# A recurrent-convolution and gated-MLP kernel: loads spread over two queues, four roots on ScalarE, a dummy Silu, eight banks for products and a new written order

## The chip, the cores and the metric

The kernel runs on one core of a Trainium2 chip. Its engines work side by side and meet through semaphores: TensorE (PE in the profile; its weight loads are PEld), VectorE (DVE), ScalarE (ACT), GpSimd (POOL) and SyncE (SP), which here only issues DMAs. ScalarE issues some DMAs too (ACTq). The metric is the device time of one execution in microseconds (us). Times are compared by the median of the runs of one kernel. The profile is of one execution, and its times count from the first instruction of the span.

## The reference

The input x is 2048 rows of 512, in bf16. What is computed:

```python
xn = layernorm(x)                                   # over the 512 columns
k_shift = sum_t  k[row - t, :] * shift_k[:, t]      # four taps
kv  = k_shift * v
y   = irfft(rfft(kv, 4096) * rfft(ssm_k, 4096))[:2048] + kv * ssm_D     # per column
s   = xn * y
h   = gelu(xn @ w_gate) * (xn @ w_up)               # 512 -> 1792
g   = silu(h @ w_down)                              # 1792 -> 512
out = x + s * g
```

## The kernel before, in words

**The MLP.** The rows are in four quarters (q0 to q3) of 512 rows, four row tiles each. For every quarter and each of 14 chunks of 128 hidden columns, a *unit* makes two products of four matmuls (gate and up, line 649), a Gelu on ScalarE (line 1216) and a multiplication on VectorE, either from PSUM (line 1225) or, where ScalarE first copies up out of PSUM, from SBUF (line 1222). The *down* product of a row tile is 14 matmuls in three pieces (4, 5, 5). For q0 to q2 a Tanh (line 1257) and a multiplication (line 1259) follow, which make the Silu and write G; the last quarter is done with the Silu itself (line 1265). The order of the quarters is q0, q1, q3, q2 with parts of q3 mixed in.

**The norm.** For each row tile VectorE takes statistics (lines 872, 873). For tiles 0 and 1, ScalarE takes a root (line 885) and VectorE the reciprocal (886); for tiles 2 and 3, and for the later quarters, GpSimd takes a power of -0.5 (line 889). q0 is transposed by TensorE; q1 to q3 by a transposing DMA on SyncE's queue (line 911, `xnT<-XN`).

**The convolution** is a transform over 4096 points in two stages, as matrix products. The filter (Hn) is loaded in four pieces; VectorE transposes each (line 940). TensorE makes the first stage of the filter in eight *H* stages (line 980), each of which takes four PSUM banks; ScalarE copies out, VectorE adds (line 988), and ScalarE's queue stores to DRAM (ZH). For the input, VectorE makes the four taps per quarter with 2048-wide operations (lines 1028, 1032, 1034) and multiplies by v (line 1036, `V<-KAC,V`, the *V piece*); the taps' weights are copied by GpSimd (line 1009, SKB). Sixteen *K* products (line 969) follow, and their stores (ZK) on SyncE's queue. The second stages run on 32 x 32 tiles (line 1051): eight of the filter, eight of the input, eight *inverses*, each with two aligned pairs of banks. The inverses are stored (ZI) and read back (BI) once all are there, then eight last products (y, line 1300) and the tail on VectorE (lines 1309, 1317, 1329, 1267, 1268). The table of the second stage (TF) is made by GpSimd: two products (line 755), a sum (758), four turned copies (642, 643); it also does one small *fold* (947).

**The order.** All work is cut into 801 numbered tasks. The string SEQ gives the order in which they are written; a task goes to the list of its engine, or with the letter b to its second choice, and each engine works its list in order. Semaphore waits are derived from what a task reads and writes. Loads are tasks too, each in the queue that its line names. LAND holds assumed landing times; with them the builder works out which PSUM bank a task gets, and nothing else depends on them. PSUM has eight banks: products take single ones (pool `psF`, at most NF_BANKS at a time), the transforms aligned pairs.

Numbers of the tasks that the prediction names: 14, 15 the two table products; 16 their sum; 76 the turned copies; 127 to 130 the tap copies; 54 the fold; 454, 455, 456 variance, power and bias of q1; 138, 146, 154, 162 the V pieces; 206 to 208 and the like the K stages; 125, 90, 110 the additions and 126, 91, 111 the stores of H stages 7, 0, 4; 652 to 658 variance to normalised rows of q3, 659 its transposing DMA; 560 to 566 and 567 the same of q2; 732, 735, 741 three of the multiplications of line 1309; 345 the last inverse; 13 the row copies of FT; 75 the table of Gelu.

GpSimd's list before: 2 4 3 5 70 73 127 130 129 128 455 54 14 15 16 76 653 561.

Of the kernel before, what the change touches and what calls it, by code (L numbers as in the profile page):

```python
# [26 lines left out]
SEQ = (  # L27
# [23 lines left out]
)  # L51
NF_BANKS = 4
ISSUE = 470.0
LAND = {"x0_0": 3350, "x0_1": 3900, "wg0": 5000, "wu0": 5700, "x0_2": 6200, "wg1": 7900, "wu1": 9400, "h0": 10700, "h1": 12000, "wg2": 13500, "wu2": 15000, "h2": 16300, "h3": 17600, "D": 18000, "kz": 10800, "x1": 19500, "sk": 21500, "kh1": 23000, "kh113": 23200, "k0": 24600, "wg3": 26100, "wu3": 27600, "k1": 29000, "wd0": 31800, "k2": 33200, "wd1": 35700, "v0": 37200, "v1": 38600, "k3": 40000, "v2": 41400, "v3": 42700}
W_XT, W_SW, W_BK, W_BH, W_ZI, W_BI, W_ZK, W_MI, W_G1 = 850000, 690000, 685000, 688000, 310000, 575000, 600000, 329000, 150000
# [5 lines left out]
N_SPLIT = 2  # L61
N_ROOT = 2
UNITS = [(0, 6), (0, 8), (0, 10), (0, 12), (1, 0), (1, 2), (1, 4), (1, 6), (1, 8), (1, 10), (1, 12), (1, 1), (1, 3), (1, 5), (1, 7), (1, 9), (1, 11), (1, 13)]
# [357 lines left out]
def build_kernel(nc, A_q, A_k, A_v, A_shift_k, A_ssm_k, A_ssm_D, B_w_gate, B_w_up, B_w_down, out):  # L421
    with ExitStack() as es0:
# [100 lines left out]
        trk = Trk(nc, block)  # L523
# [21 lines left out]
        R_id = res("ident", ident[:])  # L545
        R_cols, R_col1, R_col2 = (res(f"COLS{i}", COLS[:, i:i + 1]) for i in range(3))
        R_st = [res(f"st{t}", stats[:, t, :]) for t in range(NT)]
# [78 lines left out]
        def load(name, out_ap, in_ap, w_res, w_buf, nbytes, ring="SP", r=(), rb=()):  # L626
            sem = dsem("d_" + name)
            last_load[0] = S.add([("loads", ISSUE)], lambda e: dma(ring, out_ap, in_ap, sem, r, w_res), r=rb, w=w_buf, nbytes=nbytes, land=float(LAND[name]))

# [133 lines left out]
        def gelu_table(e):  # L763
            trk.op("ACT", lambda h: h.activation(COLS[:, 1:2], COLS[:, 0:1], ACTF.Gelu_apprx_tanh), r=[R_cols], w=[R_col1])

        def sines(e):
            sin(F1, C32[:].rearrange("p a c -> p (a c)"), [R_C32], R_F1)
            sin(TAB[:], PH[:], [R_PH], R_TAB)
            gelu_table(e)
# [51 lines left out]
        def load_x0(t):  # L821
            ts = slice(*((0, 1), (1, 2), (2, 4))[t])
            load(f"x0_{t}", X[:, ts, :], x_dr[:, ts, :], R_X[ts], bX[0][ts], 131072 * (ts.stop - ts.start))

# [5 lines left out]
        def load_h(k, ring):  # L830
            load(f"h{k}", Hn[:, k, :], h_dr[:, k, :], [R_Hn[k]], [bHn[k]], 524288, ring)
# [28 lines left out]
        for what in ORDER.split():  # L860
            if what[0] == "x" and len(what) == 3:
                load_x0(int(what[2]))
                continue
            {"k": load_k, "v": load_v, "w": lambda i: load_w(i, ("ACT", "ACT") if i == 0 else ("SP", "SP")), "x": load_x, "d": load_wd, "h": lambda i: load_h(i, "SP"), "s": load_taps, "D": load_d}[what[0]](int(what[1:]))

# [65 lines left out]
        d_out = []  # L931
        gu_tasks = [[] for _ in range(NQ)]
        down_tasks = [[] for _ in range(NQ)]

# [253 lines left out]
        def unit(q, m):  # L1188
# [10 lines left out]
            if q == 0 and m < N_HALF:  # L1199
# [15 lines left out]
            gu_tasks[q] += [tg, tu]  # L1215
            op([("ACT", act(512))], lambda e, h: h.activation(GE[:, g.slot, :], bank(pg), ACTF.Gelu_apprx_tanh), r=[pg], w=[g],  # L1216
               rr=lambda: R_bank(pg), ww=lambda: [R_GE[g.slot]], after=[t_gelu] if q == 0 else [])
            af = (down_tasks[q - 2] if q >= 2 else []) + (s1_tasks["H"] if q == 1 else [])
# [9 lines left out]
        def down(q):  # L1228
            for jt in range(4):
                t = 4 * q + jt  # L1230
                cols = [(0, DM)] if t < NT - 1 else [(0, 384), (384, DM)]
                for c0, c1 in cols:
# [23 lines left out]
                    if q < NQ - 1:  # L1256
                        op([("ACT", act(n))], lambda e, h, g=g, pc=pc: h.activation(g, pc(), ACTF.Tanh, scale=0.5), r=[p], w=[bt],  # L1257
                           rr=lambda p=p: R_bank(p), ww=rg, after=h_tr_tasks + (h2_tasks if q >= 2 else []))
                        op([("DVE", dve(512, 1))], lambda e, h, g=g, pc=pc: h.scalar_tensor_tensor(out=g, in0=g, scalar=1.0, in1=pc(), op0=ALU.add, op1=ALU.mult),
                           r=[p, bt], w=[bG[t // 2]], rr=lambda p=p, rg=rg: R_bank(p) + rg, ww=rg)  # L1260
                        continue
# [3 lines left out]
                    op([("ACT", act(n))], lambda e, h, g=g, pc=pc: h.activation(g, pc(), ACTF.Silu), r=[p], w=[bt],  # L1265
                       rr=lambda p=p: R_bank(p), ww=rg, after=zh_tasks + h2_tasks)
                    op([("DVE", dve(n, 2))], lambda e, h, g=g, u=u: h.tensor_tensor(g, g, u, ALU.mult), r=[bt, bS[t // 2]], w=[b2], rr=rg + [R_XN[t]], ww=rg)
# [36 lines left out]
        for j in range(8):  # L1304
# [6 lines left out]
            else:  # L1311
# [6 lines left out]
               rr=lambda by=by, R_g=R_g: [R_BO[by.slot], *R_g], ww=R_g)  # L1318

        down(NQ - 1)  # L1320


# [64 lines left out]
```

## Time and profile before

| | |
|---|---|
| median of 3 runs | 189.59 us (189.29 to 191.28) |
| profiled execution | 189.26 us, span 187.4 us |
| TensorE busy | 178.4 us (95%) |
| VectorE busy | 172.5 us (92%) |
| ScalarE busy | 138.4 us (74%) |
| GpSimd busy | 19.6 us (10%) |
| granted TensorE clock | 1.0 in every slice |

A row of a timeline reads: start in us, busy us, engine, line, operation, what is written `<-` what is read, partitions x elements and type, count, and in brackets the idle time just before it and what ended that. A row of waits reads: engine, line `<-` what it waited for: us in all, times, longest. A row of windows reads: the window, its length, the busy time of the engine with its count, the granted clock, the DMA share and GB/s. Operations of one engine overlap a little at their ends, so that the step from one start to the next is about 0.1 us shorter than the busy time.

### The profile page before, as it was taken

How to read it: one execution, taken by the hardware profiler on the slowest of the kernel's cores; microseconds unless marked ns; L12 is line 12 of the kernel's file. 1: busy time of each engine (PE TensorE's matmuls, PEld its weight loads, DVE VectorE, ACT ScalarE, POOL GpSimd, SP SyncE). 2: the span in 40 equal slices, each digit the busy share in tenths (PEclk: the TensorE clock that was granted, in tenths of full speed). 3: DMA queues.
4: the chain of work that ended last, by engine and by line, in shares of the span. 5: the costliest groups of instructions: out<-in, count | busy, mean ns of one | idle time of the engine just before them, and what ended most of it. 6: DMA issues, size and time to landing. Idle time of an engine off the chain costs nothing.

```text
span 187.4 us, 3808 instructions
## 1 busy us (share of the span) xinstructions
PE 178.4 (95%) x1522; PEld 77.8 (42%) x1522; DVE 172.5 (92%) x251; ACT 138.4 (74%) x200; POOL 19.6 (10%) x31
## 2 busy tenths in 40 slices
PE   8699999989499999999999999999999999999993
PEld 3464444344244433343443443343333434445552
DVE  5898999999999999999778999999999998769995
ACT  3697797985387999987847479798887977451771
POOL 4200135991000000002200000000000000000000
PEclk9999999999999999999999999999999999999999
DMA  5999999999756689357979959689942416599248
GB/s 164 337 373 403 317 364 366 405 352 223 237 205 243 229 286 287 132 191 259 292 220 283 320 205 327 220 263 286 351 159 115 168 59 224 162 371 394 98 153 284
DMA packets 38684, 48.38 MB, mean 258 GB/s; under 512 B 9484, under 2 KB 28428, under 8 KB 38667
## 3 DMA queue, kind: packets, MB, share of 16 engines
q1 hardware_dynamic: 31082, 39.23, 65.3%
q10 hardware_dynamic: 7584, 8.91, 13.5%
q8 instruction: 12, 0.20, 0.4%
q14 instruction: 6, 0.04, 0.1%
HBM read 27.39 MB, written 14.68 MB: 225 GB/s over the span
## 4 chain that ended last, share of the span: by engine, by line
PE 66%; DVE 21%; DMA 6%; SPq 3%; POOL 2%; issue 1%; DVEq 0%
PE psall L649 55%; DMA Hn<-in_A_ssm_k_dram 6%; PE psall L1051 6%; DVE KTM L1032 3%; SPq L622 3%; DVE KAC L1034 3%; PE psall L969 2%; DVE G L1329 2%; DVE G L1317 2%; DVE HTr L940 2%; PE psall L1246 2%; POOL mv L889 2%; DVE HT L1225 1%; DVE HT L1222 1%; DVE X L988 1%
## 5 line engine op out<-in xcount | busy, mean ns | idle before, releaser
L649 PE MATMUL psall<-xnT,Wg 128*128 128x512 bf16 (+1 forms) x248 | 56.6, 359 | 0.0
L649 PE MATMUL psall<-xnT,Wu 128*128 128x512 bf16 (+1 forms) x248 | 56.3, 359 | 0.2 <-ACT xnT L640 0.2
L649 PE MATMUL psall<-Wd,HT 128*128 128x512 bf16 (+1 forms) x182 | 40.3, 368 | 0.9 <-DVE HT L1225 0.9
L1216 ACT ACTIVATE GE<-psall 128x512 bf16<-128x512 f32 x54 | 31.6, 608 | 11.7 <-PE psall L649 10.0
L649 PEld LDWEIGHTS psall<-xnT,Wu 128*128 128x128 bf16 x248 | 22.5, 98 | 26.4 <-issue 1.3
L649 PEld LDWEIGHTS psall<-xnT,Wg 128*128 128x128 bf16 x248 | 21.6, 98 | 26.5 <-issue 3.8
L1225 DVE TENSOR_TENSOR HT<-psall,GE 128x512 bf16<-128x512 f32 x36 | 24.2, 682 | 5.5 <-PE psall L649 5.1
L649 PEld LDWEIGHTS psall<-Wd,HT 128*128 128x128 bf16 x182 | 16.2, 98 | 21.5 <-issue 2.5
L640 ACT ACTIVATE BO<-psall 128x1024 bf16<-128x1024 f32 x19 | 19.0, 1028 | 6.0 <-PE psall L1051 3.2
L1154 DVE TENSOR_TENSOR HSW<-KB,HSW 128x2048 bf16<-128x2048 bf16 x16 | 19.5, 1218 | 0.4 <-ACT KB L640 0.3
L640 ACT ACTIVATE HSW<-psall 128x1024 bf16<-128x1024 f32 x15 | 14.6, 1030 | 3.0 <-PE psall L1051 1.8
L640 ACT ACTIVATE KB<-psall 128x1024 bf16<-128x1024 f32 x14 | 14.0, 1035 | 3.7 <-PE psall L1051 3.7
L1032 DVE TENSOR_TENSOR KTM<-KK,SKB 128x2048 bf16<-128x2048 bf16 x12 | 15.3, 1272 | 0.0
L1034 DVE TENSOR_TENSOR KAC<-KAC,KTM 128x2048 bf16<-128x2048 bf16 x12 | 14.8, 1237 | 0.1
L1246 PE MATMUL psall<-Wd,HT 128*64 128x512 bf16 (+1 forms) x112 | 12.5, 366 | 0.0
L889 POOL TENSOR_TENSOR mv<-mv,NHALF 128x4 f32<-128x4 f32 (+1 forms) x5 | 6.1, 1212 | 58.8 <-DVE mv L883 53.4
L872 DVE BATCH_NORM_STATS2 stats<-X 128x6 f32<-128x512 bf16 x16 | 10.6, 677 | 1.1 <-DMA X<-in_A_q_dram 1.0
L1257 ACT ACTIVATE G<-psall 128x512 bf16<-128x512 f32 x12 | 7.1, 599 | 6.0 <-PE psall L649 5.5
L640 ACT ACTIVATE X<-psall 128x1024 bf16<-128x1024 f32 x8 | 8.2, 1028 | 4.0 <-PE psall L980 3.9
L640 ACT ACTIVATE U__73<-psall 128x512 bf16<-128x512 f32 x18 | 10.9, 617 | 0.3 <-PE psall L649 0.3
L640 ACT ACTIVATE AST<-psall 128x1024 bf16<-128x1024 f32 x10 | 10.1, 1029 | 1.1 <-PE psall L969 0.9
L1154 DVE TENSOR_TENSOR KB<-KB,HSW 128x2048 bf16<-128x2048 bf16 x8 | 9.6, 1219 | 0.1
(95 smaller groups left out, 189.7 us busy)
## 6 DMA issues: line engine op xcount, KB each, us to landing
BH<-ZH SPq DMA_DIRECT2D x8, 512.0 KB, 4.4
HSW<-HSW SPq DMA_DIRECT2D x16, 256.0 KB, 2.7
BK<-ZK SPq DMA_DIRECT2D x8, 512.0 KB, 6.0
ZI<-BO ACTq DMA_DIRECT2D x16, 256.0 KB, 2.5
BI<-ZI SPq DMA_DIRECT2D x8, 512.0 KB, 8.1
ZK<-AST SPq DMA_DIRECT2D x6, 512.0 KB, 3.0
Hn<-in_A_ssm_k_dram SPq DMA_DIRECT2D x4, 512.0 KB, 9.1
KK<-in_A_k_dram SPq DMA_DIRECT2D x4, 512.0 KB, 11.9
```

The lines of the kernel that those rows point to most:

```text
L640: return h.activation(o, i, ACTF.Copy, scale=scale)
L649: return h.matmul(o, lhsT=l, rhs=r, start=st, stop=sp)
L872: t_stats[t] = op([("DVE", 670.0)], lambda e, h, t=t: h.bn_stats(stats[:, t, :], X[:, t, :]), r=[bX[q][t % 4]], w=[bst[t]], rr=[R_X[t]], w ...
L889: t_pw = op([("POOL", 2500.0 if q else 600.0)], lambda e, hd, ts=ts, n=n: hd.tensor_tensor(mv[:, ts, 3:4], mv[:, ts, 2:3], NHALF[:, 0:n, : ...
L1032: op([("DVE", dur)], lambda e, h, j=j, m=m: h.tensor_tensor(KTM[:, m.slot, :, :], kk(j), sk(j), ALU.mult), r=need + [bSKB[j], a], w=[m], r ...
L1034: op([("DVE", dur)], lambda e, h, m=m: h.tensor_tensor(KAC[:, a.slot, :, :], KAC[:, a.slot, :, :], KTM[:, m.slot, :, :], ALU.add), r=[m], ...
L1051: trk.op("PE", lambda h: h.matmul(ps(s, i)[b, :], lhsT=wt(col)[a, :], rhs=data(col)[a, :], start=n < 16, stop=n >= len(todo) - 16, tile_po ...
L1154: return hd.tensor_tensor(pair(KB, *(2 * DM * z for z in slots())) if to else x, k, x, ALU.mult)
L1216: op([("ACT", act(512))], lambda e, h: h.activation(GE[:, g.slot, :], bank(pg), ACTF.Gelu_apprx_tanh), r=[pg], w=[g], rr=lambda: R_bank(pg ...
L1225: op([("DVE", dve(512, 1))], lambda e, h: h.tensor_tensor(HT[:, q % 2, m, :], bank(pu), GE[:, g.slot, :], ALU.mult), r=[pu, g], w=[bHT[q][m]],
L1246: trk.op("PE", lambda h, m=m, i=i, c=c: h.matmul(pc()[c, :], lhsT=HT[:, q % 2, m, 128 * jt + 64 * i:128 * jt + 64 * i + 64], rhs=Wd[:, m, ...
L1257: op([("ACT", act(n))], lambda e, h, g=g, pc=pc: h.activation(g, pc(), ACTF.Tanh, scale=0.5), r=[p], w=[bt], rr=lambda p=p: R_bank(p), ww= ...
```

## The change

- Row 1 of x is loaded on ScalarE's queue instead of SyncE's, and the first gate weights (g0) on SyncE's instead of ScalarE's.
- All four row tiles of q0 take their root on ScalarE (N_ROOT 4), and none a power on GpSimd. The load of the Gelu table waits for all four.
- Products may hold up to eight PSUM banks (NF_BANKS 8).
- A dummy Silu of one column is a task of its own (754; later numbers move up by one), behind the last 24 activations of the Gelu table; the Silus of the last quarter follow it.
- LAND and SEQ are new. GpSimd's list becomes: 2 4 5 3 127 129 15 130 14 128 54 455 16 76 653 561 (70 and 73 are now reciprocals on VectorE). The copies of PSUM that go to VectorE instead of ScalarE are others, nine where there were ten.

```diff
 SEQ = (
...
-    "454 455 54 408 95 117 409 423 118 403 139 416 410 411 119 417 42 418 456 14b 15b 133 419 420 105 43 106 412 112 426 425 134 460b 421 457b "
-    "135 44 120 458b 459b 136 137 16b 113 96 436 431 140 427 437 114 428 107 432 438 433 138 115 141 429 121 45 430 142 108 143 122 109 110 441 "
...
+    "62 28 71 29 72 83 73 74 363 351 84b 85 75 366 86b 10 370 356 368 369 367 357 30 371 358 31 32 33 34 359 11 354 355 386 382 387 360 12 388 "
+    "372 383 50 35 399 390 51 361 389 373 404 384 385 127 13b 52 391 395 400 53 392 393 402 406 401 405 396 36 37 97 394 378 446 397 407 129 398 "
+    "98 452 379 92 38 15b 380 130 99 450 448 381 374 453 14b 93 375 128 376 131 102 94 408 422 409 100 403 451 132 449 447 103 39 101 377 40 104 "
+    "133 454 410 411 424 117 41 54 134 118 42 417 423 119 419 418 425 413 414 455 135 456 420 421 412 415 416 112 426 441 436 136 457b 458b 437 "
...
+    "562 564 565 659 541 566 684 712 179b 545 563b 246 170 546 686 713 259 714 680 682 247 715 567 181 685 248 664 681 666 551 687 250 260 249 "
...
 )
-NF_BANKS = 4
+NF_BANKS = 8
...
-N_ROOT = 2
+N_ROOT = 4
...
+        def silu_table(e):
+            trk.op("ACT", lambda h: h.activation(COLS[:, 3:4], ONE[:, 0:1], ACTF.Silu), w=[R_col3])
...
-            load(f"x0_{t}", X[:, ts, :], x_dr[:, ts, :], R_X[ts], bX[0][ts], 131072 * (ts.stop - ts.start))
+            load(f"x0_{t}", X[:, ts, :], x_dr[:, ts, :], R_X[ts], bX[0][ts], 131072 * (ts.stop - ts.start), "ACT" if t == 1 else "SP")
...
-  ... "w": lambda i: load_w(i, ("ACT", "ACT") if i == 0 else ("SP", "SP")) ...
+  ... "w": lambda i: load_w(i, ("SP", "ACT") if i == 0 else ("SP", "SP")) ...
...
-                       rr=lambda p=p: R_bank(p), ww=rg, after=zh_tasks + h2_tasks)
+                       rr=lambda p=p: R_bank(p), ww=rg, after=zh_tasks + h2_tasks + [t_silu])
...
+        t_silu = S.add([("ACT", 1480.0)], silu_table, w=[B("silu")], after=gelu_set[-24:])
         down(NQ - 1)
```

More of the change, by code (lines that the diff above doesn't have):

```diff
@@ L27 @@
 SEQ = (
[23 rows of a table removed]
[23 rows of a table added]
 )
-NF_BANKS = 4
+NF_BANKS = 8
 ISSUE = 470.0
-LAND = {"x0_0": 3350, "x0_1": 3900, "wg0": 5000, "wu0": 5700, "x0_2": 6200, "wg1": 7900, "wu1": 9400, "h0": 10700, "h1": 12000, "wg2": 13500, "wu2": 15000, "h2": 16300, "h3": 17600, "D": 18000, "kz": 10800, "x1": 19500, "sk": 21500, "kh1": 23000, "kh113": 23200, "k0": 24600, "wg3": 26100, "wu3": 27600, "k1": 29000, "wd0": 31800, "k2": 33200, "wd1": 35700, "v0": 37200, "v1": 38600, "k3": 40000, "v2": 41400, "v3": 42700}
+LAND = {"x0_0": 3150, "x0_1": 3350, "wg0": 5000, "wu0": 5400, "x0_2": 6200, "wg1": 7900, "wu1": 9400, "h0": 10750, "h1": 12050, "wg2": 13550, "wu2": 15050, "h2": 17300, "h3": 18600, "D": 18500, "kz": 12300, "x1": 20300, "sk": 22200, "kh1": 23500, "kh113": 23700, "k0": 24900, "wg3": 26400, "wu3": 27900, "k1": 29200, "wd0": 31800, "k2": 33100, "wd1": 36600, "v0": 37900, "v1": 39200, "k3": 40700, "v2": 42100, "v3": 43500}
 W_XT, W_SW, W_BK, W_BH, W_ZI, W_BI, W_ZK, W_MI, W_G1 = 850000, 690000, 685000, 688000, 310000, 575000, 600000, 329000, 150000
@@ L545, in build_kernel @@
         R_id = res("ident", ident[:])
-        R_cols, R_col1, R_col2 = (res(f"COLS{i}", COLS[:, i:i + 1]) for i in range(3))
+        R_cols, R_col1, R_col2, R_col3 = (res(f"COLS{i}", COLS[:, i:i + 1]) for i in range(4))
         R_st = [res(f"st{t}", stats[:, t, :]) for t in range(NT)]
@@ L863, in build_kernel @@
                 continue
-            {"k": load_k, "v": load_v, "w": lambda i: load_w(i, ("ACT", "ACT") if i == 0 else ("SP", "SP")), "x": load_x, "d": load_wd, "h": lambda i: load_h(i, "SP"), "s": load_taps, "D": load_d}[what[0]](int(what[1:]))
+            {"k": load_k, "v": load_v, "w": lambda i: load_w(i, ("SP", "ACT") if i == 0 else ("SP", "SP")), "x": load_x, "d": load_wd, "h": lambda i: load_h(i, "SP"), "s": load_taps, "D": load_d}[what[0]](int(what[1:]))
         t_stats = [None] * NT
@@ L932, in build_kernel @@
         gu_tasks = [[] for _ in range(NQ)]
+        gelu_set = []
         down_tasks = [[] for _ in range(NQ)]
@@ L1215, in unit @@
             gu_tasks[q] += [tg, tu]
-            op([("ACT", act(512))], lambda e, h: h.activation(GE[:, g.slot, :], bank(pg), ACTF.Gelu_apprx_tanh), r=[pg], w=[g],
-               rr=lambda: R_bank(pg), ww=lambda: [R_GE[g.slot]], after=[t_gelu] if q == 0 else [])
+            gelu_set.append(op([("ACT", act(512))], lambda e, h: h.activation(GE[:, g.slot, :], bank(pg), ACTF.Gelu_apprx_tanh), r=[pg], w=[g],
+                               rr=lambda: R_bank(pg), ww=lambda: [R_GE[g.slot]], after=[t_gelu] if q == 0 else []))
             af = (down_tasks[q - 2] if q >= 2 else []) + (s1_tasks["H"] if q == 1 else [])
@@ L1256, in down @@
                     if q < NQ - 1:
-                        op([("ACT", act(n))], lambda e, h, g=g, pc=pc: h.activation(g, pc(), ACTF.Tanh, scale=0.5), r=[p], w=[bt],
-                           rr=lambda p=p: R_bank(p), ww=rg, after=h_tr_tasks + (h2_tasks if q >= 2 else []))
+                        gelu_set.append(op([("ACT", act(n))], lambda e, h, g=g, pc=pc: h.activation(g, pc(), ACTF.Tanh, scale=0.5), r=[p], w=[bt],
+                                           rr=lambda p=p: R_bank(p), ww=rg, after=h_tr_tasks + (h2_tasks if q >= 2 else [])))
                         op([("DVE", dve(512, 1))], lambda e, h, g=g, pc=pc: h.scalar_tensor_tensor(out=g, in0=g, scalar=1.0, in1=pc(), op0=ALU.add, op1=ALU.mult),
```

39 rows, old and new, of the table SEQ are left out of this document.

## The prediction

> **What bounds the kernel now.** I read the page first, then TensorE's waits, then VectorE in a window, then the places where the two meet.
>
> ```profile
> PE 178.4 (95%) x1522; PEld 77.8 (42%) x1522; DVE 172.5 (92%) x251; ACT 138.4 (74%) x200; POOL 19.6 (10%) x31
> PE 66%; DVE 21%; DMA 6%; SPq 3%; POOL 2%; issue 1%; DVEq 0%
> PE psall L980 <- DVE G L1259: 2.4, 1, 2.4
> PE psall L649 <- DVE HT L1225: 0.9, 1, 0.9
> PE psall L980 <- DVE HTr L940: 0.2, 1, 0.2
> 17.70:86.00 68.30, 67.79 (x91) 1.00 0.84 274
> ```
>
> The page and the chain of waits (first two lines) name TensorE. But the three waits that TensorE has after its first products all name VectorE, and come to 3.5 us. The last line is VectorE in the window 17.7 to 86.0 us: 67.79 of 68.30 us busy. So up to 86 us VectorE sets the clock. TensorE has slack there, and spends it in those three waits.
>
> How tight the two are is seen where TensorE takes over what VectorE made: the shifted key times value (V, line 1036) goes into the K transforms (line 969), and the normalised third quarter goes through a transposing DMA (line 911) into its products.
>
> ```profile
> 59.34 1.22 DVE L1036 TENSOR_TENSOR V<-KAC,V 128x2048 bf16<-128x2048 bf16 x1
> 60.98 0.82 PE L969 MATMUL psall<-V,FT 64*128 64x512 bf16 x6
> 70.21 1.23 DVE L1036 TENSOR_TENSOR V<-KAC,V 128x2048 bf16<-128x2048 bf16 x1
> 72.20 0.82 PE L969 MATMUL psall<-V,FT 64*128 64x512 bf16 x6
> 85.42 0.15 DVE L883 TENSOR_SCALAR mv<-mv 128x4 f32<-128x4 f32 x1
> 89.89 3.40 SPq L911 DMA_TRANSPOSE xnT<-XN  x1
> 97.39 3.93 SPq L911 DMA_TRANSPOSE xnT<-XN  x1
> DMA to landing us min/median/max: 6.1/6.3/6.4
> 96.44 1.02 PE L649 MATMUL psall<-xnT,Wg 128*128 128x512 bf16 x4
> 105.15 1.03 PE L649 MATMUL psall<-xnT,Wg 128*128 128x512 bf16 x4
> ```
>
> The second V piece ends at 60.56 and its K matmuls follow within the group at 60.98. The third ends at 71.44, and TensorE comes at 72.20: 0.76 us of slack. The transposed last quarter lands at 89.89 + 6.4 = 96.3, and is used at 96.44: none. The third quarter's, issued at 97.39, lands at 103.5 and is used at 105.15: 1.6. From there TensorE runs without a wait in the list to the tail. So the end moves by as much as these meetings move, and not by what TensorE alone could save.
>
> **The change part by part.**
>
> *The front (queues, roots).* Row 1 of x comes sooner, g0 later, and four roots on ScalarE replace two powers on GpSimd. VectorE gains a copy and a reciprocal, and loses one small addition. None of it reaches the end, because of this row:
>
> ```profile
> 17.73 3.94 DVE L940 STREAM_TRANSPOSE HTr<-Hn 128x1024 int32<-128x1024 int32 x2 [0.57 <-DMA Hn<-in_A_ssm_k_dram]
> ```
>
> VectorE waits there 0.57 us for the third piece of the filter. That piece has the same place in SyncE's queue and the same bytes ahead of it, as x0_1 (128 KB) leaves that queue and g0 (256 KB) joins it while ScalarE's sheds the difference. The new order has the same count of product-multiplications before this transpose, so VectorE starts its saturated stretch at 17.7 as before. Price at the end: 0. If the cover goes, what is late is up to 0.57 us.
>
> The table of Gelu now waits for all four roots, where it waited for two. Queued behind it on ScalarE are the first Gelus, the sines and the six row copies of FT. FT is first needed when the fourth filter transpose is done, 17.73 + 3.94 = 21.67, and I find some 3 us of room by adding up ScalarE's list. Price: 0.
>
> *The dummy Silu.* The load is early already:
>
> ```profile
> 167.20 1.28 ACT L1265 ACT_TABLE_LOAD   x1
> 172.29 0.60 ACT L1265 ACTIVATE G<-psall 128x512 bf16<-128x512 f32 x1 [3.81 <-PE psall L1246]
> ```
>
> It ran five microseconds before the first Silu, in idle time. In the new list four evictions of y stand ahead of the first Silu, so without the dummy the load would come among them; with it, it comes where it was. Price: 0, and 0.2 us for the extra activation, before y is there. The Trainium skill (ScalarE: Activation LUTs, "What ACT_TABLE_LOAD costs") has a switch of tables at about 2.66 us, 1.38 of it a drain, which would speak against putting the load ahead of y. The row above shows 1.28 and the measurement decides; by the page y's first copy would be 1.4 us later, still ahead of the reuse of its banks, and the sum the same.
>
> *GpSimd's order.* This is where I see the gain. VectorE is slowed between 33 and 44 us:
>
> ```profile
> 33.25 0.38 DVE L894 SCALAR_TENSOR_TENSOR NB__68<-mv 128x4 f32<-128x4 f32 x1 [0.31 <-POOL mv L889]
> 33.55 1.21 DVE L1034 TENSOR_TENSOR KAC<-KAC,KTM 128x2048 bf16<-128x2048 bf16 x1
> 34.68 1.53 DVE L988 TENSOR_TENSOR X<-X 128x1024 bf16<-128x1024 bf16 x1
> 36.14 1.26 DVE L1222 TENSOR_TENSOR HT<-U__73,GE 128x512 bf16<-128x512 bf16 x1
> 37.33 0.68 DVE L1225 TENSOR_TENSOR HT<-psall,GE 128x512 bf16<-128x512 f32 x1
> 37.93 1.69 DVE L1032 TENSOR_TENSOR KTM<-KK,SKB 128x2048 bf16<-128x2048 bf16 x1
> 39.54 0.63 DVE L1222 TENSOR_TENSOR HT<-U__73,GE 128x512 bf16<-128x512 bf16 x1
> 40.09 1.42 DVE L1034 TENSOR_TENSOR KAC<-KAC,KTM 128x2048 bf16<-128x2048 bf16 x1
> 41.44 0.90 DVE L988 TENSOR_TENSOR X<-X 128x1024 bf16<-128x1024 bf16 x1
> 42.26 1.43 DVE L1032 TENSOR_TENSOR KTM<-KK,SKB 128x2048 bf16<-128x2048 bf16 x1
> 43.73 1.23 DVE L1034 TENSOR_TENSOR KAC<-KAC,KTM 128x2048 bf16<-128x2048 bf16 x1
> ```
>
> The same forms later, with GpSimd idle, and GpSimd's own rows:
>
> ```profile
> 55.53 1.22 DVE L1028 TENSOR_TENSOR KAC<-KK,SKB 128x2048 bf16<-128x2048 bf16 x1
> 56.66 0.69 DVE L988 TENSOR_TENSOR X<-X 128x1024 bf16<-128x1024 bf16 x1
> 57.27 0.68 DVE L1259 SCALAR_TENSOR_TENSOR G<-G,psall 128x512 bf16<-128x512 bf16 x1
> 57.86 1.22 DVE L1034 TENSOR_TENSOR KAC<-KAC,KTM 128x2048 bf16<-128x2048 bf16 x1
> 61.60 0.75 DVE L1222 TENSOR_TENSOR HT<-U__73,GE 128x512 bf16<-128x512 bf16 x2
> 62.28 1.22 DVE L1034 TENSOR_TENSOR KAC<-KAC,KTM 128x2048 bf16<-128x2048 bf16 x1
> ...
> 22.16 1.86 DVE L872 BATCH_NORM_STATS2 stats<-X 128x6 f32<-128x512 bf16 x3
> 22.58 2.40 POOL L1009 COPY SKB<-SKR 128x512 bf16<-128x512 bf16 x4 [13.33 <-DMA SKR<-in_A_shift_k_dram]
> 33.56 3.56 POOL L755 TENSOR_TENSOR TM<-TAB 128x512 f32<-128x512 f32 x2
> 37.20 1.33 POOL L758 TENSOR_TENSOR TF<-TM,TM 128x512 bf16<-128x512 f32 x1
> ```
>
> Read by starts, a clean 2048-wide operation takes 1.13 us of VectorE (55.53 to 56.66), a 1024-wide one 0.61, one from PSUM 0.59, a 512-wide one from SBUF 0.34 (0.68 for two). The nine operations that start from 33.55 and are done with at 43.73 would so take 4 x 1.13 + 2 x 0.61 + 2 x 0.34 + 0.59 = 7.0 us, against 10.18. So 3.2 us are lost. Of these, 0.85 + 0.85 = 1.7 fall on the two operations at 34.68 and 36.14 that stand beside GpSimd's two table products (line 755, 33.56 to 37.12), and 1.5 on those beside the sum and the turned copies behind it.
>
> The new list puts the two table products before the power of the second quarter, between the tap copies: some 24 to 28 us. VectorE's list there is product-multiplications from PSUM and row statistics. What it costs under those no row shows. The nearest for nothing: three statistics beside the tap copies took 1.86 us, 0.62 each, not slowed. The nearest for the full price: 1.7. I take nothing, because it is the same kind of VectorE work; but the last tap copy and the fold now meet two-input operations, between 0 and one copy's 0.6: I take 0.3. The wait of 0.31 for the power (33.25) goes, since three long operations now stand between the two. The 1.5 for the sum and turned copies stays. Together 1.7 - 0.3 + 0.3 = 1.7 us, ends 0 and 2.0.
>
> By the Trainium skill (SBUF — State Buffer, "Who interferes with whom") an operation with one SBUF input outside the two-port modes does not contend with GpSimd, one with two SBUF inputs does, and the later one is blocked whole. The rows agree where they show it (1.53 against 0.69). By that rule the moved products cost nothing under statistics and PSUM work, which is the end I took; the sum by it is the same 1.7, and it is why the other end has the smaller chance.
>
> *VectorE's order to the meetings.* Ahead of the second V piece the new list has the same work (one 0.34 for another): 59.34 - 1.7. Ahead of the third one more 0.34: 70.21 + 0.34 - 1.7 = 68.85, ending at 70.08. Ahead of the last quarter's variance one statistics less (0.62): 85.42 - 0.6 - 1.7 = 83.1.
>
> *TensorE's order.* The three waits are met by other orders of down and filter stages; with the eight banks free to any product, its position at the K stage would be 3.5 us earlier if nothing held it. It is held: the third V piece allows 0.76 - 0.34 + 1.7 = 2.1. The transposing DMA of the last quarter allows 0.6 + 1.7 = 2.3 by VectorE. Ahead of it on SyncE stands the last K store, whose matmuls now come behind one more down piece (five matmuls); TensorE being 2.1 early covers that to within a few tenths, and one of the K store's copies leaves VectorE's list here. So 2.1.
>
> *ScalarE's stores.* Three stores of the filter's transform (tasks 126, 91, 111) stand on ScalarE's queue for additions on VectorE (125, 90, 110) that now come behind multiplications of G. Queued behind them are the first Gelus and copies of the second quarter, and TensorE's banks wait for those. I find ScalarE held until about 56 us, where TensorE is waiting for the second V piece (57.6 + 1.2) anyway. Price: 0 with that cover; without it, up to the 2.1.
>
> *Behind 96 us.* TensorE has the same matmuls and the same number of changes of tile shape (77, counted in both lists), so no work is saved. Three multiplications of G (line 1309) move from the tail into VectorE's middle. Two of them, 1.2 us, now stand before the rows of the third quarter: its transpose lands later by that against VectorE; VectorE's 1.7 and the 1.6 of slack cover it. The last inverse is the 201st of TensorE's 236 tasks in both lists, so the loads behind it start at the same distance from the end. Price 0; that the 2.1 is carried to the end is the weakest step, since some hundred new hand-overs have no row.
>
> **The sum.** The profiled execution took 189.26 us (span 187.4); 189.26 - 2.1 = 187.15. It lies 0.33 under the median 189.59, so on the median's scale 187.5.
>
> **The rivals.**
> - *All of TensorE's waits go*: 189.59 - 3.5 = 186.1. It needs the V pieces 1.4 us earlier still; VectorE's 67.79 of 68.30 speaks against it. Chance 0.08.
> - *GpSimd's work only collides elsewhere*: the 1.7 stays lost, and only 0.76 - 0.34 = 0.4 remains: 189.2. For it: GpSimd's work is no smaller, and any two-input operation that slips by a microsecond meets it. Chance 0.25.
> - *Slower: products take the pairs of banks.* Before, products held at most four banks; now they may hold all eight, and each 32-row stage (16 transforms, 8 inverses) needs two free aligned pairs. If each waits w for an eviction, it costs 24 w; it decides from 0.17 us, where 24 x 0.17 = 4.1 eats the 2.1 and 1.9 (1%) more. At 0.2 us, 4.8 - 2.1 = 2.7 slower: 192.3. For it: ScalarE is 74% busy, and every pair that holds a Gelu waits for it. Against: stages and products alternate as before, and TensorE had no wait at a 32-row stage. Chance 0.12.
> - *It does not do what it says*: so with the queues, roots and dummy, as priced; this is in the forecast.
>
> **The numbers.** The forecast (0.55) has its own range 186.9 to 188.8, from a gain at the third V piece between 0.8 and 2.6. A measurement of this kernel tells 1% (1.9 us) from no change, so faster is below 187.7: some 0.36 of the forecast and the first rival, 0.44. Within 1%: the rest of the forecast and the second rival, 0.44. Slower 0.12. The range 186.0 to 190.2 takes in the forecast, the second rival and the near half of the first.
>
> **What would show it.** Right: no TensorE wait on line 1259; table products on GpSimd near 25 us, and the first 1024-wide addition and 512-wide multiplication behind them near 0.7 and 0.4; V pieces near 57.6 and 68.9; first product of the last quarter near 94.3; Silu's table where it was. Wrong: V pieces where they were; TensorE waits at line 1051; or a gain at 96 us that is lost by 168.

## The result: 3.8% slower

The changed kernel took 197.84 us (median of four runs, 196.13 to 198.88). The kernel before took 190.44 us beside it. The ratio is 1.038, with a 95% interval of 1.027 to 1.049. The forecast was 187.5 us, and slower had 0.12: the sign is wrong, and the miss is 10.3 us. The profiled execution took 196.13 us, the least of the four and 6.9 us more than the one before; its span is 194.3 us. Medians here and below are over all executions of a kernel; the ratios leave out those that took over 1.5% more than its fastest.

Line numbers of the changed kernel are 3 or 4 higher than before (1036 is 1040, 969 is 973, 1051 is 1055, 988 is 992, 872 is 875). First the page of the changed kernel, its busy times and its chain of waits; then its VectorE in the window of the prediction:

```profile
PE 181.1 (93%) x1522; PEld 78.5 (40%) x1522; DVE 170.5 (88%) x252; ACT 139.8 (72%) x202; POOL 17.9 (9%) x29
PE 56%; DMA 22%; DVE 10%; ACT 8%; issue 2%; SPq 0%; ACTq 0%
17.70:86.00 68.30, 64.45 (x414) 26.93 (x413) 64.17 (x84) 55.11 (x83) 13.79 (x13) 0.98 0.75 242
```

DMA had 6% of the chain; now it has 22%. VectorE, which was full to 86 us, is now busy for 64.17 of 68.30 us. The waits of the changed kernel, by engine, line, and what ended them:

```profile
PE psall L649 <- ACT XN L640: 2.9, 1, 2.9
PE psall L649 <- DMA xnT<-XN: 1.3, 1, 1.3
PE psall L1055 <- ACT AST L640: 1.0, 1, 1.0
PE psall L649 <- ACT BO L640: 0.7, 1, 0.7
PE psall L1055 <- ACT BO L640: 0.6, 1, 0.6
ACT XN L640 <- DMA ZH<-XN: 4.0, 1, 4.0
DVE XN L992 <- ACT XN L640: 3.0, 1, 3.0
```

TensorE waits for no Tanh product of VectorE any more (that wait was 2.4 us). It waits for ScalarE, and ScalarE for stores: a copy out of PSUM needs a staging buffer whose store to DRAM has not landed. The longest DMA pieces of the chain of the changed kernel (start, us, what) are three such places and the input of the last quarter:

```profile
45.07 9.35 DMA ZH<-XN
...
84.91 6.11 DMA ZK<-AST
...
93.61 7.86 DMA xnT<-XN
...
133.40 5.87 DMA ZI<-BO
```

The meetings that the prediction named, in the changed kernel's timeline:

```profile
60.49 1.22 DVE L1040 TENSOR_TENSOR V<-KAC,V 128x2048 bf16<-128x2048 bf16 x1
72.43 1.22 DVE L1040 TENSOR_TENSOR V<-KAC,V 128x2048 bf16<-128x2048 bf16 x1
101.52 1.69 PE L649 MATMUL psall<-xnT,Wg 128*128 128x512 bf16 x7 [1.27 <-DMA xnT<-XN]
164.10 0.62 PE L1055 MATMUL psall<-HSW,MI 32*32 32x512 bf16 x24 [0.61 <-ACT BO L640]
```

Forecast were 57.6, 68.9 and 94.3 for the first three. Before, the last inverse ran from 157.10 to 157.75; here it ends at 164.10 + 0.62 = 164.7. So in this trace 5.1 us are lost at the first product of the last quarter, 7.0 by the last inverse, and nothing behind it.

Where the DMAs of these places stand shows in SyncE's queue. First the kernel before, then the changed one (start, us that the issue took):

```profile
25.76 3.81 SPq L622 DMA_DIRECT2D V<-in_A_v_dram  x2
29.61 0.43 SPq L622 DMA_DIRECT2D KK<-in_A_k_dram  x1
39.62 3.46 SPq L911 DMA_TRANSPOSE xnT<-XN  x1
43.13 1.04 SPq L622 DMA_DIRECT2D V<-in_A_v_dram  x2
44.22 1.89 SPq L1062 DMA_TRANSPOSE MI<-TFB  x1
...
74.98 5.48 SPq L622 DMA_DIRECT2D ZK<-AST  x2
```

```profile
39.15 2.78 SPq L914 DMA_TRANSPOSE xnT<-XN  x1
41.98 1.33 SPq L622 DMA_DIRECT2D V<-in_A_v_dram  x1
43.37 1.61 SPq L622 DMA_DIRECT2D KK<-in_A_k_dram  x1
45.02 1.18 SPq L622 DMA_DIRECT2D V<-in_A_v_dram  x2
...
73.65 1.67 SPq L1066 DMA_TRANSPOSE MI<-TFB  x1
80.14 1.14 SPq L1066 DMA_TRANSPOSE G<-FT  x1
82.48 1.20 SPq L1066 DMA_TRANSPOSE MI<-TFA  x1
...
84.36 0.51 SPq L622 DMA_DIRECT2D ZK<-ASX  x1
```

Two things in it are not in the prediction. The loads of the second V piece and of the last k piece (tasks 44 and 45) now stand behind the transposing DMA of the second quarter, which waits for its rows until 39.15; so 2 MB of loads are issued at 42 to 46 us, in the middle of the filter's stores, where it was 1 MB before. And the three small transposing DMAs of the second stage's tables (tasks 165, 163, 164), which were spread out, now stand one behind the other, and each waits for the one before: they hold the queue from 73.65 to 83.7, with the K stores behind them.

### The profile page after: what moved, and what is told of

It reads as the page before. It is cut to its first block, busy times and chain, and to the rows that moved or that the text cites. A ratio compares the mean times of both kernels' runs of the same rounds, so it can differ in the third digit from the quotient of the medians.

```text
span 194.3 us, 3811 instructions
## 1 busy us (share of the span) xinstructions
PE 181.1 (93%) x1522; PEld 78.5 (40%) x1522; DVE 170.5 (88%) x252; ACT 139.8 (72%) x202; POOL 17.9 (9%) x29
## 4 chain that ended last, share of the span: by engine, by line
PE 56%; DMA 22%; DVE 10%; ACT 8%; issue 2%; SPq 0%; ACTq 0%
PE psall L649 46%; DMA ZI<-BO 5%; DMA ZH<-XN 5%; DMA xnT<-XN 4%; PE psall L1055 4%; DMA ZK<-AST 3%; ACT BO L640 3%; DMA X<-in_A_q_dram 3%; PE psall L1250 2%; DMA ZH<-X 2%; PE psall L973 2%; DVE G L1334 1%; PE psall L1304 1%; DVE KAC L1038 1%; ACT XN L901 1%
## 5 line engine op out<-in xcount | busy, mean ns | idle before, releaser
L649 PEld LDWEIGHTS psall<-xnT,Wu 128*128 128x128 bf16 x248 | 22.0, 98 | 29.8 <-issue 3.9
L649 PEld LDWEIGHTS psall<-xnT,Wg 128*128 128x128 bf16 x248 | 22.2, 99 | 29.1 <-issue 3.1
L640 ACT ACTIVATE BO<-psall 128x1024 bf16<-128x1024 f32 x20 | 20.2, 1024 | 9.4 <-PE psall L1304 3.1
L640 ACT ACTIVATE KB<-psall 128x1024 bf16<-128x1024 f32 x15 | 14.8, 1024 | 1.6 <-PE psall L1055 1.5
L1036 DVE TENSOR_TENSOR KTM<-KK,SKB 128x2048 bf16<-128x2048 bf16 x12 | 14.6, 1216 | 0.0
L640 ACT ACTIVATE HSW<-psall 128x1024 bf16<-128x1024 f32 x13 | 13.1, 1026 | 2.1 <-PE psall L1055 1.9
L640 ACT ACTIVATE XN<-psall 128x1024 bf16<-128x1024 f32 x10 | 10.2, 1022 | 5.6 <-DMA ZH<-XN 4.0
L1263 DVE SCALAR_TENSOR_TENSOR G<-G,psall 128x512 bf16<-128x512 bf16 x12 | 8.1, 680 | 2.2 <-ACT G L1261 2.2
L1181 DVE TENSOR_TENSOR HSW<-HSW 128x2048 bf16<-128x2048 bf16 x8 | 9.7, 1218 | 0.0
```

Of the source, the lines that this page charges most:

```text
L640: return h.activation(o, i, ACTF.Copy, scale=scale)
L649: return h.matmul(o, lhsT=l, rhs=r, start=st, stop=sp)
L1036: op([("DVE", dur)], lambda e, h, j=j, m=m: h.tensor_tensor(KTM[:, m.slot, :, :], kk(j), sk(j), ALU.mult), r=need + [bSKB[j], a], w=[m], r ...
L1181: return hd.tensor_tensor(x, x, y, ALU.add)
```

## The experiments

Each diff shows the order of the tasks that it touches, in the list of one engine. Runs 1 to 4 were on one chip, 5 to 8 and 9 to 12 on another in two sessions; the kernel before ran beside each of the three groups (medians 190.68 to 190.81), and the ratios are against that. Each run has one trace, so a reading from it is of one execution. Runs 1 to 7 look for the loss, 8 and 9 for the forecast gain, 10 to 12 at the small parts.

**1. The loads ahead of the transposing DMA, in the changed kernel.**

```diff
-43 461 44 45 46 47 49
+43 44 45 461 46 47 49
```

> The changed kernel with one edit: in SyncE's queue the loads of the second V piece and the last k piece (tasks 44, 45) stand ahead of the transposing DMA of the second quarter (461), as before the change. Theory A (late loads slow the filter's stores): in the changed kernel these loads are issued at 42 to 46 us behind the transposing DMA that waits for its rows; 2 MB of them share the DMA engines with the store of 45.07, which takes 9.35 us, and ScalarE waits 4.0 us for its staging buffer, TensorE 2.9, VectorE 3.0. With the edit that store lands within about 4 us, the waits are under 1 us together, the V pieces start near 57.5 and 69.5, and the time is about 196.1 - 3.0 = 193 us, not all the way back as the later queue order stays. Rival B (the stores are slow because the transposing DMA itself moves beside them, or because ScalarE's own list puts them together): the store at 45 still takes over 7 us, the V pieces stay at 60.5 and 72.4, and the time stays within 1 us of the changed kernel, 195 to 199.

Measured: 195.32 us (193.71 to 197.14), ratio 1.017 (1.008 to 1.026), about 2% less than the changed kernel. The V pieces start at 59.70 and 70.79, 0.8 and 1.6 us sooner, TensorE's wait for the copies of XN is 0.7 + 0.4 and ScalarE's for the store 1.9. But the store, now issued at 46.24, still takes 7.39 us. Theory A has the sign; that these two loads are the whole of it is refuted, and rival B keeps a part.

**2. The small transposing DMAs back to their places, in the changed kernel.**

```diff
-47 49 225 48 215 210 171 165 163 164 166 220
+47 165 49 163 225 48 164 215 210 171 166 220
```

> The changed kernel with one edit: the three small transposing DMAs of the second stage's tables (tasks 165, 163, 164), which stand one behind the other at 73.65 to 83.7 us in SyncE's queue, go back to about the places they had before the change: 165 behind the last V load, 163 and 164 behind the two loads of x. Theory C (the three hold SyncE's queue, each waits for the landing of the one before, and the K stores behind them are late): the K stores that were issued at 84.4 to 85.4 go out near 76 to 82, the transposing DMA of the last quarter goes out at 91 to 92 instead of 93.6, and the time is 1.5 to 2.5 us under the changed kernel's: about 194. Rival D (that transposing DMA is held by VectorE's variance, 87.49 against 85.42 before, anyway): no more than 0.5 us.

Measured: 194.74 us, ratio 1.021 (1.013 to 1.030). The K store that was issued at 84.36 goes out at 81.44, the transposing DMA of the last quarter at 92.46 instead of 93.61, and its first product starts at 98.83 instead of 101.52. Theory C holds, though that DMA was expected at 91 to 92; rival D falls.

**3. Both.** The diffs of 1 and 2 together.

> Both edits of SyncE's queue in the changed kernel (loads first, small transposing DMAs early). If theories A and C hold and are all that went wrong with the forecast, the other steps stand: V pieces near 57.5 and 69.5, first product of the last quarter near 94.5, and 187.5 us, or up to 189. If they hold but new hand-overs behind 96 us cost as well, 190 to 192. If neither holds, 195 to 199.

Measured: 193.62 us (190.99 to 195.06), ratio 1.011 (1.005 to 1.016). The first product of the last quarter starts at 96.27, as before the change (96.44). But the last inverse is late all the same. From the timeline of this run, TensorE at the last inverse, and from its chain of waits the place where it was lost:

```profile
161.84 0.62 PE L1055 MATMUL psall<-HSW,MI 32*32 32x512 bf16 x24 [0.90 <-ACT BO L640]
```

```profile
128.15 7.01 DMA ZI<-BO
...
135.18 1.03 ACT BO L640
...
136.26 3.02 PE psall L649 x8
```

The last inverse ends at 161.84 + 0.62 = 162.5, against 157.10 + 0.65 = 157.75 before the change: with both queues mended 4.7 us are still lost, all behind 97 us. A store of an inverse issued at 128.15 takes 7.01 us, ScalarE waits for its buffer, TensorE for ScalarE. Here the prediction had put a price of 0. The traced execution took 193.88 us, where the fastest of the ten took 190.99, so 4.7 us is more than the run loses as a rule: the ratio says 1.1%, some 2 us.

**4. The opposite edit of 1, in the kernel before.**

```diff
-43 44 45 461 46 47
+43 461 44 45 46 47
```

> The kernel before with the one opposite edit: the loads of the second V piece and the last k piece (44, 45) stand behind the transposing DMA of the second quarter (461). Theory A: these loads are issued near 43 to 45 us instead of 29; the filter's stores of 43 to 55 us take longer by some us, ScalarE waits for staging buffers, and the time is 191 to 193.5 us. Rival B: the loads land in time for their use, nothing waits, 189 to 190.5.

Measured: 191.43 us (190.55 to 193.38), ratio 1.004 (1.000 to 1.008), inside the range of theory A. The trace is of the slowest of the ten executions. A copy of ScalarE in its timeline, and the time to landing of the store that was issued at 43.76:

```profile
53.36 1.02 ACT L640 ACTIVATE X<-psall 128x1024 bf16<-128x1024 f32 x1 [5.11 <-PE psall L649]
```

```profile
DMA to landing us min/median/max: 9.5/9.5/9.5
```

The copy starts when that store lands (43.76 + 9.5 = 53.3). The row puts the wait down to TensorE, but the copy's matmuls had ended at 50.87, so the store is the likelier cause. In this trace the V pieces start 2.5 and 3.9 us later (61.85 and 74.06; the first of the four, ahead of this copy, already 0.5) and the first product of the last quarter 4.1 us later (100.57). So late loads can cost the old order too; by the ratios they cost it 0.4%, and the changed order 2% (run 1).

**5. The stores of the inverses early, on top of 3.** The changed order lets eight stores (ZI) stand up to some 70 places of SEQ behind the copies that they store (268 and 270 are stored by 269 and 271, and so on). In ScalarE's list:

```diff
-268 270 283 271 282 296 294 269 284 295 307 309 297
+268 270 269 271 283 284 282 296 294 297 295 307 309
...
-322 323 308 320 321 335 310 333 336 334
+308 310 322 323 320 321 335 336 333 334
```

> The run with both edits of SyncE's queue, and one more: on ScalarE's list each store of an inverse (ZI) stands behind the next activation after the copy that it stores, where the changed order had let eight of them stand up to 70 tasks later. Theory H (staging buffers come free late): there the store of bo4_0, copied at 118.3 us, went out at 137.6, and the stores of 127.7 and 128.2 went out into four 512 KB loads and took 4.4 and 7 us, so that ScalarE waited 1.8 us for a buffer and TensorE 1.9 + 0.9 us, and the clock fell to 0.84 in 130 to 140 us. With the edit no TensorE wait on the copies of BO stays, the last inverse ends near 158.5 and the time is 3 to 4.5 us under that of both edits: 188.5 to 190.5. Rival I (the products hold the banks that the 32-row stages need, in eight banks): the TensorE waits between 130 and 165 us stay over 2 us in sum and the time is within 1 us.

Measured: 190.19 us, ratio 1.000 (0.996 to 1.004), by the ratios 1.1% or some 2 us less than both queue edits, where 3 to 4.5 us were expected (the medians differ by 3.4, but are of two chips). The last inverse of this run, and the one wait that TensorE has for another engine behind 96 us:

```profile
157.59 0.65 PE L1055 MATMUL psall<-HSW,MI 32*32 32x512 bf16 x32
```

```profile
PE psall L1055 <- ACT GE L1220: 0.3, 1, 0.3
```

Theory H holds, with a smaller size than expected. Rival I, in which products sit in the banks that the 32-row stages need, is refuted: the only wait of that kind is 0.3 us. The stores themselves are no faster (median 4.1 us to landing against 2.5 in run 3, longest 7.8); they are only issued early enough that nobody waits.

**6. The other two V loads late, on top of 5.** Their V pieces come at 68 and 79 us. (The diff has the task numbers of the other runs; the last k load now comes behind these two, so this kernel's own numbers for the three differ.)

```diff
-44 45 461 46 47 165 49 163
+44 45 461 165 49 46 47 163
```

> The run before this in the list (queue edits and ZI stores early), and one more: the loads of the third and fourth V piece (1 MB, needed at 69 and 81 us) go out behind the load of x at 61 us instead of at 42 to 45. Theory A (loads beside the filter's stores slow them): the store of 45 us lands within 5 us instead of 8.5, ScalarE's wait of 3.0 us for that buffer falls under 1, the second V piece starts near 57.6 and the time falls by 1 to 2 us, to 187.5 to 189. Rival J (it is the transposing DMA of the second quarter at 39.1 that delays the store): the store still takes over 7 us and the time stays within 0.5 us.

Measured: 187.47 us, ratio 0.988 (0.981 to 0.995). This version is faster than both kernels, and is called the best version below. From its timeline the V pieces, the first product of the last quarter and the last inverse:

```profile
57.26 1.21 DVE L1040 TENSOR_TENSOR V<-KAC,V 128x2048 bf16<-128x2048 bf16 x1
68.35 1.21 DVE L1040 TENSOR_TENSOR V<-KAC,V 128x2048 bf16<-128x2048 bf16 x1
93.88 1.90 PE L649 MATMUL psall<-xnT,Wg 128*128 128x512 bf16 x8
155.27 0.65 PE L1055 MATMUL psall<-HSW,MI 32*32 32x512 bf16 x32
```

And the time to landing of the filter's store that is issued near 45 us (9.35 in the changed kernel), in run 3 and here:

```profile
DMA to landing us min/median/max: 8.5/8.5/8.5
```

```profile
DMA to landing us min/median/max: 3.8/3.8/3.8
```

The loads were the cause: with all four away from the filter's stores the same 512 KB land in 3.8 us, though the transposing DMA still stands beside them. Rival J falls.

**7. The stores of the inverses early, in the changed kernel alone.** The diff of 5 without those of 1 and 2.

> The changed kernel with the ZI stores early alone, and SyncE's queue as changed. Theory H: the TensorE waits on copies of BO behind 130 us (0.7 + 0.6 in the changed kernel's trace, and 0.78 at 163) go, and the time falls by 2 to 3 us, to 194 to 195.5; the 5 us that are late at the first product of the last quarter stay. Rival I: within 1 us.

Measured: 196.27 us, ratio 1.030 (1.025 to 1.036): 0.8% below the changed kernel's ratio, less than the 2 to 3 us that were expected, and the two intervals overlap. The waits for BO are gone, but TensorE waits 3.2 us for the copies of XN in this run, the last quarter starts at 102.39, and the last inverse ends at 164.8, as in the changed kernel. In this execution what the repair gives back was lost earlier.

**8. The forecast's mechanism alone: GpSimd's table products early, in the kernel before.**

```diff
-127 130 129 128 455 54 14 15 16 76
+127 130 15 129 14 128 455 54 16 76
```

> The kernel before with one part of the change alone: GpSimd's two table products (tasks 15, 14) stand between the tap copies, ahead of the power of the second quarter, as in the changed kernel. Theory F (the forecast's mechanism): the operations of VectorE that stood beside them at 34.7 and 36.1 us are not slowed any more, nothing is slowed in their place, the second and third V pieces start 1.5 to 2 us sooner (57.6 and 68.5), and the time falls by at most that, 187.5 to 188.5 us. Rival G (GpSimd's work only collides elsewhere): the V pieces stay within 0.4 us and the time within 0.5 us of the kernel before.

Measured: 188.13 us, ratio 0.988 (0.984 to 0.993): by the ratio the whole forecast gain, from one move. VectorE's rows of this run, to be read beside those of the prediction:

```profile
24.27 0.66 DVE L1225 TENSOR_TENSOR HT<-psall,GE 128x512 bf16<-128x512 f32 x1
24.86 1.12 DVE L1222 TENSOR_TENSOR HT<-U__73,GE 128x512 bf16<-128x512 bf16 x1
...
34.16 1.01 DVE L894 SCALAR_TENSOR_TENSOR NB__68<-mv 128x4 f32<-128x4 f32 x1
...
36.22 0.90 DVE L988 TENSOR_TENSOR X<-X 128x1024 bf16<-128x1024 bf16 x1
37.05 0.61 DVE L1222 TENSOR_TENSOR HT<-U__73,GE 128x512 bf16<-128x512 bf16 x1
```

The addition and the multiplication that took 1.53 and 1.26 us take 0.90 and 0.61. Multiplications from PSUM are not slowed beside the table products (0.66 at 24.27 and 0.67 at 26.50; 0.64 at 21.92, where GpSimd is idle), but the one from SBUF at 24.86 is (1.12 against 0.4), and the tiny bias operation at 34.16 takes 1.01 instead of 0.38, as it now meets the sum. The V pieces of this run start 0.9 us sooner (58.46 and 69.33), where theory F had 1.5 to 2. The rest of the gain comes with the granted clock: its mean is 0.998 or more in all six executions of this run, and 0.98 to 0.99 in twelve of the 17 of the kernel before beside them (median 190.74); against the other five, which show 1.00 (median 189.35), the gain is 1.2 us. Why the clock is kept here is open; TensorE's wait for the Tanh product is 1.3 us instead of 2.4 in this trace.

**9. And that mechanism taken out of the best version.** The two products back behind the fold and the power.

```diff
-127 129 15 130 14 128 54 455 16 76
+127 129 130 128 54 455 14 15 16 76
```

> The best run so far (all three queue edits, 187.5 us) with GpSimd's two table products back behind the fold and the power of the second quarter, as before the change. Theory F: VectorE loses some 1.7 us again between 33 and 45 us, the second V piece starts near 59 instead of 57.3, and the time is 1.5 to 2 us longer, 189 to 189.5. Rival G: no change, 187 to 188.

Measured: 188.92 us, ratio 0.993 (0.989 to 0.997). The second V piece starts at 58.49 instead of 57.26. So the move is worth at most 1.2 us of VectorE there, not 1.7. (In run 12, whose lists up to that piece are those of the best version, it starts at 57.78, so 0.5 us of this can be the difference of two executions.)

**10. Two roots back on GpSimd, in the best version.**

```diff
-N_ROOT = 4
+N_ROOT = 2
```

> The same best run with two of the four roots of the first quarter back as powers on GpSimd (N_ROOT 2). The prediction's price of the four roots is 0: within 0.5 us, and VectorE's saturated stretch starts at the same time within 0.3 us. Rival: the front counts, since VectorE is full from 17.7 us on: 0.5 to 1 us to either side.

Measured: 188.58 us, ratio 0.992 (0.989 to 0.996). The third filter transpose, with which VectorE's full stretch begins, in this run and in the best version:

```profile
19.00 3.95 DVE L944 STREAM_TRANSPOSE HTr<-Hn 128x1024 int32<-128x1024 int32 x2
```

```profile
17.76 3.93 DVE L944 STREAM_TRANSPOSE HTr<-Hn 128x1024 int32<-128x1024 int32 x2
```

In the new order two powers on GpSimd cost 1.2 us there. The four roots only keep the start that the kernel before has with two (17.73).

**11. The first loads in their old queues, in the best version.**

```diff
-            load(f"x0_{t}", ..., "ACT" if t == 1 else "SP")
+            load(f"x0_{t}", ..., "SP")
...
-load_w(i, ("SP", "ACT") if i == 0 else ("SP", "SP"))
+load_w(i, ("ACT", "ACT") if i == 0 else ("SP", "SP"))
```

> The same best run with the second row of x back on SyncE's queue and the first gate weights back on ScalarE's. The prediction's price is 0: within 0.5 us. Rival: the first products start by some 0.5 us at another time and the end moves by as much.

Measured: 188.06 us, ratio 0.989 (0.983 to 0.995). The difference from the best version, 0.1% by the ratios, is smaller than the intervals, so no price shows. (By the medians it is 0.6 us and by the second V piece, 58.00, 0.7, little more than runs 6 and 12 differ by.)

**12. Without the dummy Silu, in the best version.**

```diff
-        t_silu = S.add([("ACT", 1480.0)], silu_table, w=[B("silu")], after=gelu_set[-24:])
```

> The same best run without the dummy Silu: the table is loaded for the first real Silu. The prediction's price is 0 to 0.2 us either way. Rival: the load of 1.28 us then stands among the copies of y and the end is 0.5 to 1.3 us later.

Measured: 189.24 us, ratio 0.995 (0.992 to 0.999). ScalarE's timeline of this run, and that of the best version:

```profile
175.32 1.28 ACT L1269 ACT_TABLE_LOAD   x1
```

```profile
166.61 1.28 ACT L767 ACT_TABLE_LOAD   x1
167.90 0.20 ACT L767 ACTIVATE COLS<-const-bfloat16-1.0 128x1 f32<-128x1 bf16 x1
```

The load stands among the copies of y, as the rival said. From the end of TensorE's last matmul to the end of the span it is now 4.3 us (183.1 to 187.4), 1.4 more than in the best version (182.6 to 185.5). The best version was timed in another session than runs 9 to 12, and where their ratios differ by half a per cent the intervals overlap; there the readings above go by the traces.

No run has the new order with fewer banks for products, so what eight banks alone are worth is not shown.

## Why the prediction was wrong

*What bounds the kernel.* Right. VectorE sets the pace to 86 us; in the best version it is busy for 67.79 of 68.30 us again, TensorE has no wait over 0.8 us, and everything moves with the V pieces.

*GpSimd's order.* The mechanism is right, and alone it is faster (run 8). The term was too large: 0.9 us at the V pieces of run 8 and at most 1.2 between runs 6 and 9, not 1.7, as part of the loss moves to the multiplication at 24.86, the addition beside the fold (0.91 us at 27.30 in run 6, where 0.69 is clean), and the bias operation (1.23 us in the changed kernel, 0.38 before), to which I had given 0.3. The Trainium skill (SBUF — State Buffer, "Who interferes with whom") divides the operations as these rows do: one input from SBUF is not slowed (0.66), two are (1.12).

*The front, the dummy.* Right as priced. The stretch starts at 17.58 (17.73 before), the table loads in idle time. Runs 10 and 12 add that the new order needs both: without the four roots it loses 1.2 us, without the dummy 1.4.

*ScalarE's stores.* Wrong, and the first large term. I had written "Price: 0 with that cover; without it, up to the 2.1". I had asked when the stores are issued, not when they land. The store of 45.07 took 9.35 us, its buffer is needed again at 50.5, and TensorE's bank hangs on that copy. The cover was none: VectorE's V piece waited for the same ScalarE (3.0 us at line 992). Without that wait the second V piece would by this sum have started at 60.49 - 3.0 = 57.5, and 57.6 was forecast.

*SyncE's queue.* Missing. I followed this queue for the first loads, the last K store and the transposes of the last two quarters, and took the rest for unchanged. Loads 44 and 45 moved past task 461, and 165, 163 and 164 moved together; both could be read in SEQ, and the landing times in the trace of before say what queues beside them. Runs 1 and 2 price each at about 2%, and they don't add up (both together 2.8%).

*TensorE's order: "covers that to within a few tenths".* The transposing DMA of the last quarter went out 3.7 us later (93.61 against 89.89), where 2.1 sooner was forecast. With the queue mended it is at 89.71 (run 3).

*Behind 96 us: "Price 0".* Wrong, and named as the weakest step. I had counted TensorE's matmuls and the place of the last inverse, which are the same, and not the stores between. Late stores of the inverses cost some 2 us by the ratios of runs 3 and 5, and 4.2 us between their traces, of which run 3's is of one of its longer executions (the last inverse ends at 162.5 in run 3, at 157.59 + 0.65 = 158.2 in run 5).

*The rivals.* The slower one had the sign but not the mechanism: TensorE waits 1.0 + 0.6 us at 32-row stages of the changed kernel for copies that wait for stores, and for a product's bank at such a stage only in run 5, 0.3. No rival had a staging buffer that a store frees late, so 0.12 for slower was too little. "GpSimd's work only collides elsewhere" is refuted by run 8 as a whole, but 0.8 of the 1.7 us stay lost there.

The miss can be followed through the traces, one execution each. The last inverse of the changed kernel ends at 164.7; with the two queue edits at 162.5, with early stores at 158.2, with late V loads at 155.27 + 0.65 = 155.9. That is 1.8 us sooner than before the change, where 2.1 were forecast, and the time is 187.47, where 187.5 was forecast. That they meet is in part luck. With the loads where they stood before the change, as the forecast had them, and the stores mended too (run 5), the ratio is 1.000. Run 6 also moves two loads that the kernel before issues at 43.13 to 59.41, a step that is in no term of the prediction. And run 8 reaches the same ratio, 0.988, with one move in the old order: no run shows a gain of the rest of the new order over that. How the loss of the changed kernel divides among the repairs is open beyond this order of them, as run 7 shows.

## What to carry to other kernels

For every list that a change rewrites, write down each DMA's place in its queue before and after, what lands beside it, and which buffer it frees: a store holds its buffer until it lands, and the filter's stores of 512 KB took between 2.7 and 9.8 us here (both in run 7) by what else was in flight. An engine that "would wait anyway" is a cover only if nothing that it waits for hangs on the engine that is late. When several repairs each give little, try them together, since the next late buffer hides the gain of the first.

## What the hardware did that was not expected

A wait of TensorE can cost half as much again afterwards. The changed kernel's wait of 2.87 us, in a table of windows and in the timeline; then the kernel before, after a wait of 2.42 us:

```profile
55.50:59.50 4.00, 3.92 (x12) 1.52 (x13) 2.89 (x5) 3.09 (x6) 0.00 (x0) 0.61 0.63 238
55.58 1.89 PE L649 MATMUL psall<-xnT,Wu 128*128 128x512 bf16 x4 [2.87 <-ACT XN L640]
```

```profile
49.70:53.50 3.80, 3.76 (x32) 1.69 (x36) 3.77 (x5) 2.43 (x3) 0.00 (x0) 1.00 0.48 136
```

The granted clock was 0.61 in the four microseconds behind the first wait, and four matmuls took 1.89 instead of 1.03 us. The twelve matmuls from 55.58 to 59.65 took 4.1 us, where twelve take 2.6 at the full clock (0.86 for four): 1.5 us more. In run 3 a wait of 1.86 us (134.40 to 136.26) was followed by 0.59 for 3.8 us, in run 7 one of 3.2 us by 0.57 for as long, and in run 4 waits of 0.43 and 1.12 us, shortly behind one of 2.43, by 0.51 for 3.4 us (56.40 to 59.80). Behind the 2.42 us of the kernel before the clock stayed at 1.00, and behind 1.5 us in run 5 too. So the length of the wait alone does not decide. The Trainium skill (TensorE: Matmul & The Clock Gate, "What's actually happening") has the clock fall after an idle window of about 3.4 us, in windows that run freely. All these waits are shorter than that, so here the measurement differs from the page; that the windows run freely could be why length alone does not decide, and no run here tests it.

Loads on SyncE's queue delay stores on ScalarE's (3.8 us against 9.35 for the same store). The Trainium skill (DMA: Bandwidth & Descriptors, "Issuing engines are not separate DMA queues") says that they run on the same 16 engines whichever engine issues them; the landing times agree.
